# The first job's third output moved ahead of TensorE's expert loop, and the blank rows written later from another buffer

## Chip, cores and metric

One core of one Trainium2 chip runs the whole program. The metric is the device time of one execution in microseconds (us); lower is better. The kernel before was timed in three runs.

## What is computed

The reference is pooled attention followed by a mixture of experts in which each token goes to one expert:

```python
k_p = k.reshape(B, H, Sp, pool, D).mean(axis=3)       # B=8, H=8, S=576, D=64, pool=8: 72 keys
v_p = v.reshape(B, H, Sp, pool, D).mean(axis=3)
attn = softmax(scale * q @ k_p.T) ;  x = attn @ v_p    # x: 4608 tokens of 512
e_idx = argmax(x @ w_gate) ;  gate_w = softmax(x @ w_gate)[e_idx]
eom = sigmoid(x @ w_output_gate)
out[mask] = gate_w * eom * (relu(x[mask] @ w1[e]) @ w2[e])   # for each of 8 experts e
```

## The kernel before

The program has two phases. The first is one scheduled stream (the TileContext): 36 tiles of 128 tokens go through scores, softmax and values, and for each group of four tiles the routing computes where each token's row belongs. GpSimd (POOL) scatters every row into a DRAM tensor `xs`, sorted by expert (`place_ids`, L489); the region of expert e starts at row e * STRIDE. The order of all this is written out by hand: `at(step, f, ...)` puts a function into a plan, and a step stands for half a tile (steps 0 to 38). Functions of one step run in the order in which they were entered.

Three of these functions matter here. `gather_early` (step BEFORE = 31) waits until the scatters of the first six groups have landed and then has SyncE (SP) load the first 384 rows of expert 0 back from `xs` (`load_rows`, four DMAs, L102). `turn_x` (from step TURNS = 34) transposes these rows on VectorE (L107, called from L527). `blank_rows` (steps 28.5 to 32, eight DMAs of SP, L224) writes 128 blank rows in front of each later expert's region and at the end of `xs`; their source is `blank`, a part of the weight staging buffer `stage[5]`, which POOL clears at step 26. SP handles its list in order, so a wait in front of one DMA holds back all behind it. `stage_in` loads pieces of weights (512 KB) into the six staging buffers, piece 5 into `stage[5]` at step 33. A second cleared buffer, `tail`, lies in `kbd[0]` (a keys buffer whose last reader is tile 31) and is cleared at step 34; `blank_tail` (L447) scatters it behind the first expert's rows at the end of the phase.

At the end of the first phase TensorE already runs the first layer of expert 0's first job and five eighths of its first output (`first_layer`, the list TAIL). A barrier of all engines (L1664) separates the phases.

The second phase is a `Block` with one program per engine, in which lists of jobs are worked off. A job is three or two tiles (384 or 256 rows) of one expert: the first layer `l1` (L1185, 96 matmuls in eight chunks f), the relu on ScalarE (L1266) and a remainder on VectorE (L1408, `low`), and the second layer `l2` (L1139, 24 matmuls per tile). The three accumulators `p_h` rotate over the chunks, so chunk f waits for the remainder of chunk f - 3 (semaphore `hl`). VectorE scales the outputs (`output`, L1400), POOL scatters them. TensorE's program starts at slot CODE = 159 of a block of 256 instructions. It finishes the first job's outputs of tiles 0 and 1 (L1236, the matmuls of L703), adds to `l1` in `begin`, and enters `looped`: `one_expert` for expert 0, then a loop of four passes over pairs of experts (L903). The first job goes through the same loop body as the others: `started` gives done > 0 for it, the body skips `l1`, waits for `y`, waits for its own outputs with `pre` (L1215), adds 2 to `l2`, and skips the two calls of `l2` for tiles 0 and 1 to reach the one for tile 2:

```python
            if done is not None:
                with eng.If(done > 0):
                    eng.wait_ge(q["pre"], 2)
                    eng.nop().then_inc(q["l2"], 2)
                with eng.Else():
                    l2(e, u, 0, job)
                    l2(e, u, 1, job)
```

In this data expert 0 has two jobs of three tiles and one of two. In the profiled run the word `rows[E + 1]` is 3, so the first job is a begun one (the nop of L1216 is in the trace).

Of the kernel before, what the change touches and what calls it, by code (L numbers as in the profile page):

```python
# [13 lines left out]
I32 = mybir.dt.int32  # L14
# [7 lines left out]
N, DM, FF, E = B * S, H * D, 1024, 8  # L22
P = 128
# [3 lines left out]
STAGES = 6  # L27
# [12 lines left out]
SENT = ROW - GATES  # L40
# [42 lines left out]
TURN = 5  # L83
FIRST = 2
CODE = 159


class Shared:
# [32 lines left out]
def attention_and_routing(ctx, tc, sh, qT, kT, v, wg, wst, xs):  # L121
    nc = tc.nc
# [5 lines left out]
    def const(shape, dt, name):  # L128
        return cp.tile(shape, dt, tag=name, name=name)
# [8 lines left out]
    kbd = [const([P, 4, 2 * KEYS], F32, f"kbd{j}") for j in range(2)]  # L138
# [3 lines left out]
    rev, first, running = const([P, E], F32, "rev"), const([P, E], F32, "first"), const([P, E], F32, "running")  # L142
# [71 lines left out]
        nc.vector.tensor_copy(running, first)  # L214
        nc.vector.tensor_copy(order, rev)

    blank = sh.stage[STAGES - 1][:, 0:SENT]

    def prepare_blank():
        nc.gpsimd.memset(blank, 0.0)  # L220
# [220 lines left out]

    close = []
    tail_at = const([P, 1], I32, "tail_at")
    tail = kbd[0].rearrange("p c n -> p (c n)")[:, 0:SENT]

    def blank_tail():
        ins = nc.gpsimd.indirect_dma_start(out=xs, out_offset=bass.IndirectOffsetOnAxis(ap=tail_at, axis=0),  # L447
                                           in_=tail.bitcast(I32), in_offset=None)
        for name in ("ids", "blank"):
            tc.declare_no_dep(ins.ins, group=name, reason="rows behind the first expert's")  # L450
        tc.add_to_no_dep_group("ids", ins.ins)
# [122 lines left out]
    def at(step, f, *args):  # L574
        plan.setdefault(step, []).append((f, args))
# [42 lines left out]
    for g in range(len(GROUPS)):  # L618
        at(sum(GROUPS[:g + 1]) + 2, lambda g: queue.append([route(g), 0, g]), g)

    at(26, prepare_blank)
    for e in range(E):
        at(28.5 + 0.5 * e, blank_rows, e + 1)
    at(34, nc.gpsimd.memset, tail, 0.0)
    at(BEFORE, gather_early)
    for k in range(WIDE):
        at(TURNS + 0.5 * k, turn_x, k)
# [138 lines left out]
def experts(st, nc, sh, wst, xs, out):  # L766
# [26 lines left out]
    q = {k: st.enter_context(nc.semaphore("m_" + k)) for k in names}  # L793
# [8 lines left out]
    def counts(v):  # L802
        trips = nc.s_assert_within(v & 15, 0, 12, skip_runtime_bounds_check_because="four bits, of 36 tiles")
        pairs = nc.s_assert_within((v >> 4) & 3, 0, 2, skip_runtime_bounds_check_because="two bits")
        return trips, pairs

    def one_expert(eng, v, e, job, slot, body, late):
        trips, pairs = counts(v)
        single, after_trips, after_pairs = v & 64, v & 128, v & 256
        for size, n in ((3, trips), (2, pairs)):  # L810
            with eng.If(n > 0):
                with eng.Fori(0, n) as i:
                    each(e, size, i, n, job, slot, body, trips, pairs, single, after_trips, after_pairs, late)
            job = eng.snap(job + n)
            slot = eng.snap(slot + n * size)
        return job, slot, trips, pairs, single

    def each(e, size, i, n, job, slot, body, trips, pairs, single, after_trips, after_pairs, late):
        body(e, size, job + i, slot + i * size, single, i if size == 3 else i + trips,
             (n - 1 - i) * 128 + after_trips if size == 3 else after_pairs - (n - 1 - i) * 256,  # L820
             1 - (n - 1 - i) - (pairs if size == 3 else 0), late, n - 1 - i)
# [52 lines left out]
    def whole(eng, r, most):  # L874
        return nc.s_assert_within(eng.snap(r), 0, most, skip_runtime_bounds_check_because="there are at most 50 slots")  # L875
# [19 lines left out]
    def looped(eng, rows, body, alone, marked):  # L895
        few = eng.alloc_register("few")
        eng.reg_mov(few, 1 - ((rows[1] >> 6) & 1))
        job, slot = one_expert(eng, rows[0], 0, 0, 0, body, None)[:2]
        begun = [eng.alloc_register(k) for k in ("job_r", "slot_r")]
        words = [eng.alloc_register(f"word{k}") for k in range(2)]  # L900
        for r, x in zip((*begun, words[0]), (job, slot, rows[1])):
            eng.reg_mov(r, x)
        with nc.Fori(0, E // 2, engines=[eng.engine]) as g:  # L903
            at = begun
            for k in range(2):
                e = nc.s_assert_within(2 * g + k, 0, E - 1, skip_runtime_bounds_check_because="experts in order")
                v = nc.s_assert_within(eng.snap(words[k]), 0, 1023, skip_runtime_bounds_check_because="counts of a few bits each")
                at = far_expert(eng, v, (e, (k + 1) % 2), whole(eng, at[0], 50), whole(eng, at[1], 56), body,
                                lambda: eng.reg_load(words[1 - k], sh.table[0:1, bass.ds(e + 2, 1)]), alone,
                                [] if k else marked, few)  # L910
            for r, x in zip(begun, at):
                eng.reg_mov(r, x)
        return whole(eng, begun[0], 50), whole(eng, begun[1], 56)

    def begin(eng, rows, names, step=None):
        with eng.If(rows[E + 1] > 2):
            for name, n in names:
                eng.nop().then_inc(q[name], n)
        if step is not None:
            with eng.Else():  # L920
                step(0)
                step(1)
                with eng.If((rows[E + 1] & 1) > 0):
                    step(2)
# [4 lines left out]
    def started(e, size, rows, nth):  # L929
        return rows[E + 1] - 2 - nth if e == 0 and size == 3 else None  # L930
# [192 lines left out]
    def _(eng):  # L1123
        mm = nc.tensor.matmul

        def parity(e):
            return e[1] if isinstance(e, tuple) else e % 2

        def split_by(e, n):
            eng.wait_ge(q["wl"], 8 * (e[0] + 1) + n - EARLY)  # L1130

        def l2(e, u, k, job, bank=None):
            w, to = sh.w2[parity(e)], p_y[k if bank is None else bank]
            for f in range(8):
                if k == 0:
                    eng.wait_ge(q["hl"], 8 * job + f + 1)
                o = DM * f
                for part, h in ((0, 0), (1, 0), (0, 1)):
                    i = mm(to, ht[:, h, f, P * k:P * k + P], w[:, part, o:o + DM],  # L1139
                           start=(f == 0 and part == 0 and h == 0), stop=(f == 7 and h == 1))  # L1140
            i.then_inc(q["l2"], 1)
# [31 lines left out]
        def l1(e, size, u, job, n):  # L1173
            w = sh.w1[parity(e)]
            eng.wait_ge(q["xl"], u + size)
            if e:
                split_by(e, 4)
            for f in range(8):
                if f >= 3:
                    eng.wait_ge(q["hl"], 8 * job + f - 2)  # L1180
                for d in range(4):
                    o = FF * d + P * f
                    to, terms = p_h[f % 3][:, 0:n], [(part, xt[:, x, d, 0:n]) for part, x in ((0, 0), (0, 1), (1, 0))]
                    for k, (part, x) in enumerate(terms):
                        i = mm(to, w[:, part, o:o + P], x, start=(d == 0 and k == 0), stop=(d == 3 and k == len(terms) - 1))  # L1185
                i.then_inc(q["l1"], 1)
# [13 lines left out]
            l2(e, u, 1, job, 2)  # L1200

        def body(e, size, job, u, single, nth, more, last, late, left):
            done = started(e, size, rows, nth)
            if done is not None:
                with eng.If(done <= 0):
                    l1(e, size, u, job, size * P)
            elif size == 3:
                l1(e, size, u, job, size * P)
            else:
                two(e, u, job, more)  # L1210
                return
            eng.wait_ge(q["y"], u + 2)
            if done is not None:
                with eng.If(done > 0):
                    eng.wait_ge(q["pre"], 2)  # L1215
                    eng.nop().then_inc(q["l2"], 2)  # L1216
                with eng.Else():
                    l2(e, u, 0, job)
                    l2(e, u, 1, job)
                    with eng.If(more > 0):  # L1220
                        eng.wait_ge(q["xl"], u + size + 3)
            else:
                if e:
                    split_by(e, 8)
                l2(e, u, 0, job)
            if done is None:
                l2(e, u, 1, job)
                with eng.If(more > 0):
                    eng.wait_ge(q["xl"], u + size + 3)
            l2(e, u, 2, job)  # L1230

        eng.addr_align(256, offset=CODE, max_nops=0)
        eng.nop().then_inc(q["l2"], 1)
        for k, f0 in ((0, F0), (1, 0)):
            for f in range(f0, 8):
                i = output_chunk(nc, sh, f, p_y[k], k)  # L1236
            i.then_inc(q["pre"], 1)
        rows = table(eng)

        begin(eng, rows, [("l1", 8)])  # L1240
        job, slot = looped(eng, rows, body, one, marked)
        eng.wait_ge(q["xl"], slot + 2)
        for k in ("xs", "xu"):
# [450 lines left out]
```

## Time and profile before

| | us |
|---|---|
| runs | 604.02, 605.68, 602.70 |
| median of the runs | 604.02 |
| profiled execution, device time | 600.8 |
| span of the profiled execution | 599.1 |
| TensorE busy (PE, 3345 matmuls) | 565.9 (94% of the span) |
| weight loads (PEld) | 512.2 (86%) |
| VectorE (DVE) busy | 338.8 (57%) |
| ScalarE (ACT) busy | 256.5 (43%) |
| GpSimd (POOL) busy | 227.3 (38%) |
| read from and written to HBM | 75.07 MB and 22.59 MB |

All times in the trace are us from the start of the span. A name that ends in q (PEldq, DVEq, SPq) is the sequencer of an engine, which hands instructions to the engine and can be ahead of it; a branch, a semaphore wait or a DMA issue stands there. The arrow in brackets of a timeline row names what ended the idle time before it; "issue" says that the profile shows nothing that the engine waited for.

### The profile page before, as it was taken

The page shows a single profiled execution, that of the slowest core. Times are in us where ns is not written, and L with a number is a line of the kernel's source. Part 1 is how long each engine was busy: PE and PEld are TensorE (multiplying, and loading weights), DVE is VectorE, ACT ScalarE, POOL GpSimd, SP SyncE. Part 2 cuts the span into 40 slices and gives each one's busy share as a digit, 9 for nine tenths or more (in the row PEclk, how much of TensorE's full clock was granted, in tenths as well). Part 3 has the DMA queues.
Part 4 walks back from the last instruction along what each step waited for, and adds up shares of the span by engine and source line. Part 5 has one row for each costly group of instructions (what it writes and reads, how often), then busy time and mean ns, then how long its engine had stood idle before and what let it go on. Part 6 is the DMA issues. An engine that isn't in the chain of part 4 may idle for free. (4 is left out here: it accounts for less than half of the span.)

```text
span 599.1 us, 12079 instructions
## 1 busy us (share of the span) xinstructions
PE 565.9 (94%) x3345; PEld 512.2 (86%) x3346; DVE 338.8 (57%) x777; ACT 256.5 (43%) x693; POOL 227.3 (38%) x351
## 2 busy tenths in 40 slices
PE   2999999987987999999999999999999999999996
PEld 2899898976975989889899898999898898989895
DVE  4687888986877533679384623457244741323231
ACT  2988989886343311558162311335042420202020
POOL 3937889933534513143323112311221422213131
PEclk9999999998997999999999999999999999999999
DMA  8867799888457721469855513074223303020112
GB/s 329 318 231 292 284 345 376 294 248 233 170 144 233 242 53 37 125 210 357 251 176 193 173 48 71 18 228 140 84 50 110 76 0 94 10 70 18 53 35 71
DMA packets 49694, 97.16 MB, mean 162 GB/s; under 512 B 7054, under 2 KB 31630, under 8 KB 47824
## 3 DMA queue, kind: packets, MB, share of 16 engines
q1 hardware_dynamic: 41648, 77.14, 40.3%
q0 software_dynamic: 7968, 19.24, 8.9%
q14 instruction: 60, 0.49, 0.3%
q8 instruction: 18, 0.29, 0.2%
HBM read 75.07 MB, written 22.59 MB: 163 GB/s over the span
## 5 line engine op out<-in xcount | busy, mean ns | idle before, releaser
L1266 ACT ACTIVATE ht<-p_h 128x384 fp32r<-128x384 f32 (+1 forms) x104 | 46.8, 450 | 241.6 <-PE p_h L1185 241.4
L1608 POOL DMA_INDIRECT out<-rows,dst x41 | 42.5, 1037 | 203.7 <-DVE rows L1400 196.1
L1185 PE MATMUL p_h<-xt,w1b 128*128 128x384 f32 (+1 forms) x672 | 107.9, 320 | 1.5 <-DVE ht L1408 0.9
L1408 DVE SCALAR_TENSOR_TENSOR ht<-p_h,ht 128x384 fp32r<-128x384 f32 (+1 forms) x104 | 52.1, 503 | 100.8 <-ACT ht L1266 94.5
L1185 PEld LDWEIGHTS p_h<-xt,w1b 128*128 128x128 f32 x672 | 106.6, 189 | 2.8 <-DVE ht L1408 1.2
L1139 PE MATMUL p_y<-w2b,ht 128*128 128x512 f32 x456 | 104.8, 390 | 0.0
L1139 PEld LDWEIGHTS p_y<-w2b,ht 128*128 128x128 f32 x456 | 85.4, 188 | 17.5
L1139 PE MATMUL p_y<-w2a,ht 128*128 128x512 f32 x384 | 90.9, 397 | 3.7 <-issue 3.7
L1139 PEld LDWEIGHTS p_y<-w2a,ht 128*128 128x128 f32 x384 | 73.6, 193 | 19.4 <-issue 4.2
L1185 PE MATMUL p_h<-xt,w1a 128*128 128x384 f32 (+1 forms) x576 | 85.8, 309 | 0.8 <-DVE ht L1408 0.8
L1185 PEld LDWEIGHTS p_h<-xt,w1a 128*128 128x128 f32 x576 | 85.0, 190 | 1.7 <-DVE ht L1408 1.2
L1400 DVE TENSOR_SCALAR rows<-p_y,sc 128x512 f32<-128x512 f32 x37 | 27.7, 751 | 101.1 <-PE p_y L1139 100.0
L327 ACT ACTIVATE p<-p_h,m 128x72 f32<-128x72 f32 x288 | 72.2, 378 | 16.3 <-DVE m L321 16.1
L347 PE MATMUL p_y<-vbd,pT 128*128 128x162 f32 (+3 forms) x400 | 68.8, 323 | 3.1 <-DVE xg L370 3.0
L1585 POOL DMA_INDIRECT xm<-xs,src x54 | 56.1, 1039 | 26.3 <-POOL src L1581 14.5
L347 PEld LDWEIGHTS p_y<-vbd,pT 128*128 128x128 f32 (+1 forms) x400 | 55.2, 183 | 6.6 <-DVE xg L370 3.5
L489 POOL DMA_INDIRECT xs<-xg,where x36 | 37.2, 1032 | 29.6 <-issue 9.2
L260 POOL TENSOR_TENSOR kq<-kq 128x288 f32<-128x288 f32 (+1 forms) x63 | 40.5, 672 | 12.7 <-DMA kq<-kT 12.0
L315 PE MATMUL p_h<-kbd,q_even 128*128 128x144 f32 (+1 forms) x160 | 29.5, 314 | 11.6 <-DMA q_even<-qT 8.9
L370 DVE TENSOR_TENSOR xg<-p_y,grec 128x400 f32<-128x400 f32 x72 | 36.2, 503 | 1.6
L336 PE MATMUL ptr<-ident,p 128*128 128x128 f32 x180 | 33.1, 283 | 3.6 <-ACT pT L337 1.9
L321 DVE TENSOR_REDUCE m<-p_h 128x4 f32<-128x288 f32 x72 | 32.4, 450 | 6.8 <-PE p_h L315 6.3
(190 smaller groups left out, 663.9 us busy)
## 6 DMA issues: line engine op xcount, KB each, us to landing
stage<-wst SPq DMA_DIRECT2D x64, 512.0 KB, 5.0
kq<-kT SPq DMA_DIRECT2D x7, 1152.0 KB, 13.8
rows<-xs SPq DMA_DIRECT2D x40, 192.0 KB, 6.8
rows<-v SPq DMA_DIRECT2D x8, 768.0 KB, 5.6
kq<-qT SPq DMA_DIRECT2D x4, 1152.0 KB, 9.8
rows<-v SPq DMA_DIRECT2D x8, 512.0 KB, 6.2
rows<-xs SPq DMA_DIRECT2D x64, 64.0 KB
q_even<-qT SPq DMA_DIRECT2D x3, 1152.0 KB, 8.9
```

Of the source, the lines that this page charges most:

```text
L260: nc.gpsimd.tensor_tensor(k[:, :, 0:w], k[:, :, 0:w], k[:, :, w:2 * w], op=ALU.add)
L327: nc.scalar.activation(pt[i % 3][:, o:o + KEYS], sv[:, h], AF.Exp, bias=m[:, h:h + 1])
L336: nc.tensor.transpose(tr[:, P * c:P * c + P], pt[i % 3][:, o:o + P], ident)
L347: nc.tensor.matmul(av[r0:r0 + n, o:o + COLS * (k1 - k0)], pT[:, BLOCKS[0] * a + c, r0:r0 + n], vbd[b % 2][:, k0:k1].rearrange("p h f -> p ...
L370: nc.vector.tensor_tensor(view(xg[g][:, j], h0, [[H, D + 16], [1, n]]), avv[:, :, 0:D + 16].rearrange("p h f -> p f h"), grec[g][:, j, h0: ...
L489: ins = nc.gpsimd.indirect_dma_start(out=xs, out_offset=bass.IndirectOffsetOnAxis(ap=where, axis=0), in_=x.bitcast(I32), in_offset=None)
L1139: i = mm(to, ht[:, h, f, P * k:P * k + P], w[:, part, o:o + DM], start=(f == 0 and part == 0 and h == 0), stop=(f == 7 and h == 1))
L1185: i = mm(to, w[:, part, o:o + P], x, start=(d == 0 and k == 0), stop=(d == 3 and k == len(terms) - 1))
L1266: act(ht[:, 0, f, 0:n], p_h[f % 3][:, 0:n], AF.Relu).then_inc(q["hh"], 1)
L1408: nc.vector.scalar_tensor_tensor(ht[:, 1, f, 0:n], src, 0.0, ht[:, 0, f, 0:n].bitcast(F32), op0=ALU.max, op1=ALU.subtract).then_inc(q["hl" ...
L1585: nc.gpsimd.indirect_dma_start(out=xb[:, k].bitcast(I32), out_offset=None, in_=pairs_of, in_offset=bass.IndirectOffsetOnAxis(ap=src[:, k:k ...
L1608: nc.gpsimd.indirect_dma_start(out=out, out_offset=bass.IndirectOffsetOnAxis(ap=dst[:, k:k + 1], axis=0), in_=yb[2 if k == size - 1 else k ...
```

## The change

Two edits. In the second phase, TensorE does the third output of the begun first job ahead of the loop: if the word is above 2, it adds 8 to `l1` and 2 to `l2` and runs `l2(0, 0, 2, 0)` at once; the loop over expert 0's jobs then starts at job 1, and its body has no case for a begun job. The loop over pairs of experts is pinned to slot HEAD = 142 of its block of 256 instructions. In the first phase, the blank buffer and the tail buffer become one (`kbd[0]`), cleared once at step 33, and the eight writes of blank rows move from steps 28.5 to 32 to steps 33.5 to 37.

```diff
+HEAD = 142
...
-    blank = sh.stage[STAGES - 1][:, 0:SENT]
+    blank = kbd[0].rearrange("p c n -> p (c n)")[:, 0:SENT]
...
-    tail = kbd[0].rearrange("p c n -> p (c n)")[:, 0:SENT]
...
-                                           in_=tail.bitcast(I32), in_offset=None)
+                                           in_=blank.bitcast(I32), in_offset=None)
...
-    at(26, prepare_blank)
+    at(33, prepare_blank)
     for e in range(E):
-        at(28.5 + 0.5 * e, blank_rows, e + 1)
-    at(34, nc.gpsimd.memset, tail, 0.0)
+        at(33.5 + 0.5 * e, blank_rows, e + 1)
...
-    def one_expert(eng, v, e, job, slot, body, late):
+    def one_expert(eng, v, e, job, slot, body, late, begun=0):
...
         for size, n in ((3, trips), (2, pairs)):
-            with eng.If(n > 0):
-                with eng.Fori(0, n) as i:
+            i0 = begun if size == 3 else 0
+            with eng.If(n - i0 > 0):
+                with eng.Fori(i0, n) as i:
...
-        job, slot = one_expert(eng, rows[0], 0, 0, 0, body, None)[:2]
+        first = nc.s_assert_within((rows[E + 1] >> 1) & 1, 0, 1, skip_runtime_bounds_check_because="one bit")
+        job, slot = one_expert(eng, rows[0], 0, 0, 0, body, None, first)[:2]
...
-        with nc.Fori(0, E // 2, engines=[eng.engine]) as g:
+        with nc.Fori(0, E // 2, engines=[eng.engine], head_slot={eng.engine: HEAD}) as g:
...
         def body(e, size, job, u, single, nth, more, last, late, left):
-            done = started(e, size, rows, nth)
-            if done is not None:
-                with eng.If(done <= 0):
-                    l1(e, size, u, job, size * P)
-            elif size == 3:
-                l1(e, size, u, job, size * P)
-            else:
+            if size == 2:
                 two(e, u, job, more)
                 return
+            l1(e, size, u, job, size * P)
             eng.wait_ge(q["y"], u + 2)
-            if done is not None:
-                with eng.If(done > 0):
-                    eng.wait_ge(q["pre"], 2)
-                    eng.nop().then_inc(q["l2"], 2)
-                with eng.Else():
-                    l2(e, u, 0, job)
-                    l2(e, u, 1, job)
-                    with eng.If(more > 0):
-                        eng.wait_ge(q["xl"], u + size + 3)
-            else:
-                if e:
-                    split_by(e, 8)
-                l2(e, u, 0, job)
-            if done is None:
-                l2(e, u, 1, job)
-                with eng.If(more > 0):
-                    eng.wait_ge(q["xl"], u + size + 3)
+            if e:
+                split_by(e, 8)
+            l2(e, u, 0, job)
+            l2(e, u, 1, job)
+            with eng.If(more > 0):
+                eng.wait_ge(q["xl"], u + size + 3)
             l2(e, u, 2, job)
...
-        begin(eng, rows, [("l1", 8)])
+        with eng.If(rows[E + 1] > 2):
+            eng.nop().then_inc(q["l1"], 8)
+            eng.nop().then_inc(q["l2"], 2)
+            l2(0, 0, 2, 0)
         job, slot = looped(eng, rows, body, one, marked)
```

## Rows read from the trace of the kernel before

**Rows 1.** The page's 40 slices: granted TensorE clock, in tenths.

```profile
PEclk9999999998997999999999999999999999999999
```

**Rows 2.** Waits of PE over the whole span: total, times, longest.

```profile
PE p_y L1139 <- issue: 3.7, 1, 3.7
PE p_y L347 <- DVE xg L370: 3.0, 1, 3.0
...
PE p_y L703 <- PEq L1664: 1.8, 1, 1.8
```

**Rows 3.** Waits of PE from 195 to 599 us.

```profile
PE p_h L1185 <- DVE ht L1408: 1.8, 2, 0.9
```

**Rows 4.** Timeline of PE, 140 to 262 us: start, length, instructions, idle before.

```profile
176.03 7.80 PE L703 MATMUL p_y<-w2a,ht 128*128 128x512 f32 x33 [1.80 <-PEq L1664]
187.57 8.14 PE L1139 MATMUL p_y<-w2a,ht 128*128 128x512 f32 x24 [3.74 <-issue]
195.55 16.83 PE L1185 MATMUL p_h<-xt,w1a 128*128 128x384 f32 x96
...
240.09 11.07 PE L1139 MATMUL p_y<-w2a,ht 128*128 128x512 f32 x48
```

**Rows 5.** Sequencer instructions of L1214 and L1216: ns min/median/max, first and last start.

```profile
L1214 PEldq COMPARE_BRANCH  x3: 77/218/3439, 181.4 to 209.2; - x3
...
L1216 PEldq EVENT_SEMAPHORE  x1: 51/51/51, 183.9 to 183.9; - x1
```

**Rows 6.** Windows table: length, PE, PEld, DVE, ACT, POOL, PEclk, DMA, GB/s.

```profile
187.57:192.60 5.03, 5.03 (x12) 4.01 (x13) 4.11 (x5) 3.44 (x4) 3.89 (x4) 0.50 0.34 81
```

**Rows 7.** Timeline of DVE, 136.9 to 143.5 us.

```profile
138.66 0.45 DVE L370 TENSOR_TENSOR xg<-p_y,grec 128x240 f32<-128x240 f32 x1
142.40 0.71 DVE L107 STREAM_TRANSPOSE rows<-rows 128x512 f32<-128x512 f32 x1 [3.28 <-DMA rows<-xs]
```

**Rows 8.** Timeline of SP's DMA issues, 118 to 148 us.

```profile
122.58 2.19 SPq L224 DMA_DIRECT2D xs<-stage  x3
133.50 2.07 SPq L102 DMA_DIRECT2D rows<-xs  x4
...
146.76 1.11 SPq L503 DMA_DIRECT2D stage<-wst  x2
```

**Rows 9.** Timeline of POOL, 117 to 139 us: the sixth group's last scatter.

```profile
123.62 1.34 POOL L489 DMA_INDIRECT xs<-xg,where  x1 [0.30 <-issue]
```

**Rows 10.** Issue to landing: scatters 110 to 128 and 150 to 159; L102; L224.

```profile
xs<-xg,where POOLq DMA_INDIRECT x4, 8.7
...
xs<-xg,where POOLq DMA_INDIRECT x4, 4.6
...
DMA to landing us min/median/max: 5.6/6.8/7.3
...
DMA to landing us min/median/max: 5.8/9.6/10.3
```

**Rows 11.** Timeline of DVE, 188 to 199 us.

```profile
188.43 0.69 DVE L1359 TENSOR_TENSOR xt<-p_h,xt 128x512 fp32r<-128x512 f32 x1 [0.66 <-ACT xt L1255]
...
192.97 1.41 DVE L1400 TENSOR_SCALAR rows<-p_y,sc 128x512 f32<-128x512 f32 x2
195.75 0.75 DVE L1400 TENSOR_SCALAR rows<-p_y,sc 128x512 f32<-128x512 f32 x1 [1.37 <-PE p_y L1139]
198.38 0.56 DVE L1408 SCALAR_TENSOR_TENSOR ht<-p_h,ht 128x384 fp32r<-128x384 f32 x1 [1.88 <-ACT ht L1266]
```

**Rows 12.** Timeline of ACT, 186 to 199 us.

```profile
190.18 1.05 ACT L1262 ACTIVATE w2b<-stage 128x1024 fp32r<-128x1024 f32 x1
197.85 0.49 ACT L1266 ACTIVATE ht<-p_h 128x384 fp32r<-128x384 f32 x1 [6.62 <-PE p_h L1185]
```

**Rows 13.** Sequencer instructions of L903, the head of the loop over pairs.

```profile
L903 PEldq MOVE  x1: 29/29/29, 247.4 to 247.4; - x1
```

**Rows 14.** Waits of SP's queue, 168 to 176 us.

```profile
SPq L1664 <- DMA xs<-kbd,tail_at: 2.1, 1, 2.1
```

## Prediction

> **What bounds the kernel now.** TensorE works in 94% of the span, so I looked first for the places where it does not. The clock line of the page [rows 1] shows two dents, in the 10th slice (135 to 150 us) and in the 13th (180 to 195 us). TensorE's waits name what lies there [rows 2]: 3.7 us in front of L1139 that end by "issue", 3.0 us in front of L347 that end by a DVE normalisation, 1.8 us at the barrier between the phases. From 195 us on TensorE waits 1.8 us for DVE in two pieces [rows 3] and hardly otherwise, so from there to the end the time is matmuls: what is won earlier stays won, if nothing new comes late, and an edit that slowed the matmul stream would cost in full.
>
> The first place is the start of the second phase [rows 4]. The remaining 33 matmuls of the first job's outputs run from 176.03 for 7.80 us, to 183.83; the 24 matmuls of its third output begin at 187.57. The sequencer tells what happens between [rows 5]: the wait on TensorE's own outputs (L1216) ends at 183.9, when they are done, and then comes a branch of L1214, the jump over the two outputs that need not be computed, of 3439 ns. Such branches stand elsewhere too (median 218 ns), but there the sequencer is ahead of the matmuls; here the wait has made it give up its lead, so the branch is fully exposed. [...] So 24 matmuls take 8.14 us, where 48 of the same kind at full clock take 11.07 [rows 4], that is 5.54 for 24.
>
> The second place is in the first phase. DVE stands still for 3.28 us until 142.40, waiting for the rows that `gather_early` loads, before it can transpose them [rows 7]. It then normalises late, and TensorE's 3.0 us wait follows from that [rows 2]. Backwards: SP has issued six of the eight blank writes by 124.77, but the loads only from 133.50 to 135.57 [rows 8], because they wait for the sixth group's scatters. The last of these is issued by POOL at 123.62 [rows 9]. The four of this stretch take 8.7 us to land (median); four that run from 150 to 159 us, with no blank writes around, take 4.6 [rows 10].
>
> **The change part by part.**
>
> *Third output ahead of the loop.* The wait for `pre` is gone, and so is the taken branch behind it; the new code follows the 33 matmuls in a straight line. Cost of the new instructions: one untaken branch and two increments of about 50 ns each, as at L1216 [rows 5], with the sequencer ahead of 7.80 us of matmuls: nothing. If a fetch were late in the straight line, the bound is the same 3.4 us again; below zero it cannot go, since the same 24 matmuls must run. The third output then runs from 183.83 at full clock and ends at 183.83 + 5.54 = 189.4, where before it ended at 195.55, when job 1's first layer starts [rows 4]. That is 6.2 us: 3.7 of pause and 2.5 of clock.
>
> Who is late next? Job 1's first layer needs the third tile's remainder, done at 188.43 + 0.69 = 189.1 [rows 11]: just in time, 0 to 0.1 us. Its chunks last 16.83/8 = 2.10 us [rows 4], so the fourth can start at 189.4 + 6.3 = 195.7, once DVE has done the remainder of the first. DVE has its two outputs done at 192.97 + 1.41 = 194.4; the third (0.75), whose 1.37 us wait for TensorE is now gone, ends at 195.1 to 195.6 (its register work unseen, 0 to 0.5 us); the remainder (0.56) follows at 195.7 to 196.2 [rows 11]. ACT is no limit: its split of weights ends at 191.2, and the first relu, which waited 6.62 us for TensorE [rows 12], can run at 191.5. So a new wait of 0 to 0.5 us appears in front of the fourth chunk. I take the upper end: the register work is certainly there, only its size is unseen. Sum of this part: 6.2 - 0.5 = 5.7 us, between 5.6 and 6.2.
>
> *Blocks and the pinned loop.* By my count of instructions (two per matmul, starting from slot 159) the loop over pairs starts at slot 143 of the fourth block now; HEAD = 142 puts it at the same place of the next one, so its inner branches keep their places. New is one jump over the padding when the loop is entered. The sequencer is there at 247.4 [rows 13], while the matmuls of that stretch run to 240.09 + 11.07 = 251.2 [rows 4]: 3.7 us of lead. Priced like L1214, 3.4 us, it is covered but leaves little lead; 0 to 0.8 us, and I take 0, as branches whose median is 0.2 us are the common case.
> [...]
>
> *Blank rows later.* Eight writes of 257 KB leave the stretch from 119 to 138 us. The scatters then share it with two 512 KB loads alone. I take their landing between 4.6 and 8.7 us [rows 10], so the last has landed at 128.2 to 132.3. The loads take 2.07 us to issue [rows 8] and 5.6 to 7.3 to land [rows 10]; from first issue to last landing it was 142.4 - 133.5 = 8.9. They are there at 137.1 to 141.2. DVE wants them at 139.1 (138.66 + 0.45, [rows 7]). The gain is therefore the whole 3.28 us at one end and 1.2 at the other; zero if something else holds the scatters. I take 3.3, because the stretch from 150 to 159 is the nearer row: blank writes are missing in both. DVE runs without a pause behind it, so TensorE, ACT and POOL, who all waited for DVE, move by the same amount; the lower clock of that dent costs nothing of its own, as TensorE had slack beside DVE.
>
> Where do the writes go? Their source is now cleared in POOL's queue among the scatters of the seventh group; one clearing replaces two, and POOL had idle time there: nothing. On SP they stand behind the loads and weight piece 5, which no longer waits for `stage[5]`. Two follow at once, six behind the next weight load, which waits for a split that DVE had finished by 147.9 [rows 8]. At 0.8 us each (6.45 us for the eight) the last is issued by 152.7 and, at the longest landing of 10.3 us [rows 10], down by 163. What ends the phase is the scatter of the tail rows, for which SP waits 2.1 us shortly before the barrier [rows 14], at about 173. So 10 us of cover remain; without it every microsecond would go on the barrier. The barrier's own 1.8 us stays.
>
> **Sum.** 5.7 + 3.3 = 9.0 us. Against the profiled execution: 600.8 - 9.0 = 591.8. The median of the runs is 3.2 us above that execution; I subtract from the median: 604.0 - 9.0 = 595.0 us.
>
> **Rivals.** (A) The loads come no earlier, because the scatters are slow for another reason (the weight loads, or their own descriptors). For: there are weight loads in that stretch too. Against: the 4.6 us row. Then 604.0 - 5.7 = 598.3. (B) TensorE's fetch stall only moves: into the third output or onto the entry of expert 0's loop. For: the code around it is new and expert 0's loop lies elsewhere. Against: no jump and no wait remains there. Then 604.0 - 3.3 = 600.7. (C) Slower: the loop over pairs now lies one block further on, and a branch in it misses in every pass with no lead. One exposure costs what L1214 did, 3.7 of pause and 2.5 of clock, 6.2 us; from the second on it eats the 9.0. With three, once in each later pass: 604.0 - 9.0 + 18.6 = 613.6. For: that price was paid once. Against: [rows 3], no such wait in the same loop before, whose slots are kept. (D) Neither edit does anything: 604.0. That the new branch is not taken can be left out: L1216, which only a begun job reaches, is in the trace.
>
> **How the numbers follow.** Forecast 0.72, A 0.12, B 0.08, C 0.04, D 0.04. The largest gain from the bounds is 6.2 + 3.3 = 9.5; with the 1.3 us by which the fastest run lies under the median, 593.2, and I go to 592.5 for the clock of the first dent. Upwards the range goes to B, 600.7. Half a per cent, about what a measurement of this kernel can tell from no change, is 3.0 us, so faster means below 601.0: forecast, A and half of B, 0.88. Same: the other half of B and D, 0.08. Slower: C, 0.04.
>
> **What would show it.** In the trace after: no idle in front of the third output's 24 matmuls, which take about 5.5 us, and no lower clock there; a wait of at most about half a microsecond for DVE a few chunks into job 1; DVE's transposes without a wait for rows; SP's loads issued at about 129, blank writes behind them; the barrier 3.3 us earlier, its wait still for the tail. I am wrong if a new "issue" wait stands in front of L1139 or L1185, if the loads still leave at 133, or if waits appear after 250 us in the loop over pairs.

## Result and the profile after

The kernel after takes 608.92 us (median of six runs, 606.68 to 610.04) beside 603.80 for the kernel before in the same comparison: ratio 1.0078, 95% interval 1.0053 to 1.0103. It is slower by about 5 us where 9 us less was forecast. The profiled execution took 608.39 us with a span of 606.6 (before: 600.8 and 599.1).

First the stretch that the edit of the third output aimed at, in the timeline of PE after (start, length, instructions, idle before):

```profile
176.82 7.77 PE L702 MATMUL p_y<-w2a,ht 128*128 128x512 f32 x33 [1.45 <-PEq L1652]
184.43 5.60 PE L1140 MATMUL p_y<-w2a,ht 128*128 128x512 f32 x24
190.00 6.54 PE L1186 MATMUL p_h<-xt,w1a 128*128 128x384 f32 x36
197.13 10.69 PE L1186 MATMUL p_h<-xt,w1a 128*128 128x384 f32 x60 [0.60 <-issue]
```

The third output has no pause in front and takes 5.60 us instead of 8.14 [rows 4]. From the start of the 33 matmuls to the start of job 1's first layer it is 190.00 - 176.82 = 13.18 us; before it was 195.55 - 176.03 = 19.52 [rows 4]: 6.3 us less. The small wait of 0.60 a few chunks into job 1 is there too. So this part did what was forecast, and still the program is longer. From the start of job 1's first layer to the end of the span it is 606.6 - 190.0 = 416.6 us, where before it was 599.1 - 195.55 = 403.6. Thirteen microseconds came in behind the place that was changed. The waits of PE after, from 195 to 604 us, say where (total, times, longest; before: [rows 3]):

```profile
PE p_h L1186 <- issue: 9.7, 2, 9.1
PE p_h L1186 <- DVE ht L1396: 2.2, 2, 1.4
PE p_h L1162 <- issue: 0.3, 1, 0.3
```

The 9.1 us in the timeline of PE after, 280 to 312 us:

```profile
279.74 11.49 PE L1140 MATMUL p_y<-w2a,ht 128*128 128x512 f32 x50
300.34 11.84 PE L1186 MATMUL p_h<-xt,w1b 128*128 128x256 f32 x79 [9.11 <-issue]
```

This is the second pass of the loop over pairs, in front of expert 3's first job. What the sequencer did then is in its instructions after (ns min/median/max, first and last start):

```profile
L828 PEldq COMPARE_BRANCH  x8: 66/76/2915, 243.7 to 598.0; - x8
...
L835 PEldq COMPARE_BRANCH  x6: 68/72/5821, 255.6 to 598.7; - x6
...
L904 PEldq COMPARE_BRANCH  x5: 76/208/431, 243.0 to 600.0; - x5
```

L835 is `with eng.If(trips > 0)` in `far_expert`. Expert 3 has no job of three tiles, so the sequencer jumps over that body, and this one jump, which starts at 290.0, takes 5821 ns. The matmuls in the queue end at 291.2: the lead is 1.2 us, and 4.6 us of the jump lie open. The other 4.5 us of the wait are the way from the jump's target to the first matmul: up to the next branch (L843, at 299.3) the sequencer takes 3.4 us there, where the kernel before takes 0.9 (from 293.6 to 294.4). L828 in the first pass (2915 ns) is the jump to the path for an expert with a single job; there the lead covers all but 0.3 us. L904 is the head of the loop; it has five branches where the kernel before has four. The fifth is the jump over the padding.

Of the two queues that the page names instruction, q14 moved 60 packets before and after, and q8 seven more after; the row of q8 in the table of DMA queues of before, then of after (packets, MB):

```profile
q8 instruction: 18, 0.29, 0.2%
```

```profile
q8 instruction: 25, 0.41, 0.3%
```

And the pause costs clock. The clock line of the page of after, and the windows table for the stretch of the low clock (columns as in [rows 6]):

```profile
PEclk9899999999999999999799999999999999999999
```

```profile
294.92:305.16 10.24, 4.82 (x22) 4.82 (x23) 0.62 (x2) 1.44 (x2) 3.53 (x7) 0.50 0.06 16
```

The dents of [rows 1] in slices 10 and 13 are gone and there is a new one in slice 20: 4.82 us of matmuls at 0.50, which would take 2.4 at full clock. The price of the pause that this jump begins is 9.1 + 2.4 = 11.5 us. (The dent in slice 2 belongs to an early pause at 22 us. It stands in some of the profiles and not in others, with and without either edit.)

The first phase, timeline of SP's issues after, 118 to 150 us:

```profile
130.94 2.13 SPq L103 DMA_DIRECT2D rows<-xs  x4
134.41 0.82 SPq L503 DMA_DIRECT2D stage<-wst  x2
139.97 0.95 SPq L225 DMA_DIRECT2D xs<-kbd  x2
```

The loads leave ahead of the blank writes and earlier than in [rows 8], although the work before them was late in this execution: POOL's scatter that starts at 133.0 us before starts at 137.0 here.

### The profile page after: what moved, and what is told of

Its sections match the earlier page's. It is cut to its first block, busy times and chain, and to the rows that moved or that the text cites. A ratio compares the mean times of both kernels' runs of the same rounds, so it can differ in the third digit from the quotient of the medians.

```text
span 606.6 us, 12067 instructions
## 1 busy us (share of the span) xinstructions
PE 567.3 (94%) x3345; PEld 512.3 (84%) x3346; DVE 338.5 (56%) x777; ACT 256.5 (42%) x693; POOL 226.9 (37%) x350
## 4 chain that ended last, share of the span: by engine, by line
PE 52%; issue 2%; DVE 1%; DVEq 0%; POOL 0%; ACT 0%; POOLq 0%; ACTq 0%
PE p_y L1140 26%; PE p_h L1186 25%; PE p_h L1162 1%; PE p_h L1168 0%; DVE w2b L1354 0%; DVE ht L1396 0%; POOL out L1596 0%; DVE xt L1347 0%; DVE rows L1388 0%; DVE flat L1382 0%; ACT ht L1263 0%; DVEq L1442 0%; DVEq L875 0%; DVEq L865 0%; DVEq L868 0%
## 5 line engine op out<-in xcount | busy, mean ns | idle before, releaser
L1186 PE MATMUL p_h<-xt,w1b 128*128 128x384 f32 (+1 forms) x672 | 110.0, 324 | 10.5 <-issue 9.1
L1186 PEld LDWEIGHTS p_h<-xt,w1b 128*128 128x128 f32 x672 | 108.7, 193 | 11.9 <-issue 9.7
L1140 PE MATMUL p_y<-w2a,ht 128*128 128x512 f32 x384 | 88.4, 389 | 0.0
L1140 PEld LDWEIGHTS p_y<-w2a,ht 128*128 128x128 f32 x384 | 71.8, 188 | 14.7
```

## Experiments

Each ratio is against runs of the kernel before on the same chip. Line numbers shift by a few between kernels. Slots are written block:slot in blocks of 256, the unit by which the kernel aligns TensorE's program (`addr_align(256, offset=CODE, ...)`), blocks numbered from 0 (the prediction's "fourth block" is block 3 here), and are my count of instructions. The expectations use letters: M, that the place of the loop within its block decides, to two slots; B, a loss in the first phase; S, that expert 0's loop now makes one pass instead of two and so brings less code; J, that the jump over the padding makes the loss. T and the numbered J's are explained where they first stand.

**Two slots (M).** The kernel after with HEAD = 140.

```diff
-HEAD = 142
+HEAD = 140
```

> The changed kernel with HEAD = 140 instead of 142: the loop over pairs is still entered by the jump over the padding, but lies two slots lower in its block, as in the kernel before. Theory M (missing block): in the first pass expert 1 takes the single-job path; with HEAD = 142 that path begins at slot 1 of the block after next, so the block between is never brought in, and the jump of L835 in the second pass (expert 3 has no job of three tiles) finds it missing: 9.1 us of wait and 10.2 us at half clock, some 11.5 us in all. With HEAD = 140 the path begins at slot 255 of that block and brings it in: no such wait, 608.9 - 11.5 = 597.4 us (595.5 to 599.5). Rival J (the jump into the loop itself loses what was fetched ahead, wherever it lands): the wait stays, 607 to 610. Rival B (the loss lies in the first phase, with the blank writes): 607 to 610 as well, but without the 9.1 us wait.

605.89 us, ratio 1.0066 (1.0043 to 1.0089). The sequencer's row:

```profile
L835 PEldq COMPARE_BRANCH  x6: 68/72/5765, 253.1 to 594.9; - x6
```

The wait stays at 8.3 us. M falls as it was put, with a border between slots 140 and 142.

**Without padding, first try.**

```diff
-CODE = 159
-HEAD = 142
+CODE = 116
+HEAD = 140
```

> The changed kernel with CODE = 116 and HEAD = 140: TensorE's second program starts 43 slots earlier, so the loop over pairs comes to lie at slot 140 of the fourth block of itself, as in the kernel before, and nothing is jumped over. Theory M and rival J both: no wait at L835, and the branch of L828 (2.9 us after the change) is short again: 597 us (595.5 to 599). Rival B: 607 to 610. If code116 and head140 agree within 1 us, the jump over the padding costs nothing by itself.

604.48 us, 1.0040 (1.0016 to 1.0063), L835 at 5941 ns. The edit did not do what was meant; the row of L904 still has its fifth branch:

```profile
L904 PEldq COMPARE_BRANCH  x5: 76/208/427, 240.3 to 595.4; - x5
```

Probably the padding's own branch takes a slot too, so that the head was just past the place and moved on by nearly a whole block; no run shows this. The loop is entered by a jump here as well, so the run cannot tell J from its rivals.

**One part alone: the blank rows.** The kernel before with the edits of the first phase.

```diff
-    blank = sh.stage[STAGES - 1][:, 0:SENT]
+    blank = kbd[0].rearrange("p c n -> p (c n)")[:, 0:SENT]
...
-    at(26, prepare_blank)
+    at(33, prepare_blank)
...
-        at(28.5 + 0.5 * e, blank_rows, e + 1)
-    at(34, nc.gpsimd.memset, tail, 0.0)
+        at(33.5 + 0.5 * e, blank_rows, e + 1)
```

> The kernel before with the blank rows' part alone: one buffer, cleared at step 33, writes at steps 33.5 to 37. By my prediction DVE no longer waits 3.28 us for the rows: 603.8 - 3.3 = 500.5 + 100 = 600.5 us (599.5 to 602.5). Rival B (the writes cost more in their new place, or the earlier part of the phase runs slower for them): first layer of the first job starts 1.1 us later than before, as in the profile of the changed kernel: 604.9 us or more.

597.86 us, 0.9933 (0.9905 to 0.9961). SP's issues, DVE's first transposition and two of PE's waits in this kernel:

```profile
129.09 2.22 SPq L102 DMA_DIRECT2D rows<-xs  x4
```

```profile
139.66 0.69 DVE L107 STREAM_TRANSPOSE rows<-rows 128x512 f32<-128x512 f32 x1
```

```profile
PE p_y L1137 <- issue: 2.8, 1, 2.8
...
PE p_y L347 <- DVE xg L370: 0.7, 1, 0.7
```

The loads leave at 129.09 instead of 133.50 [rows 8], the 3.28 us wait of [rows 7] is gone, the 3.0 us wait of TensorE [rows 2] has shrunk to 0.7, and the pause in front of the third output is still there, as it should be. This part gains 4.0 us by the ratio (2.3 to 5.7). B falls.

**The other part alone, with the pin.** The kernel after with the blank rows as before.

```diff
...
-    at(33, prepare_blank)
+    at(26, prepare_blank)
...
-        at(33.5 + 0.5 * e, blank_rows, e + 1)
+        at(28.5 + 0.5 * e, blank_rows, e + 1)
+    at(34, nc.gpsimd.memset, tail, 0.0)
```

> The changed kernel with the blank rows as before, so TensorE's part alone with HEAD = 142. Theory M: the third output starts at once (6 us gained) and L835 misses its block (11.5 us lost): 603.8 + 5.5 = 609.3 us (607.5 to 611). Rival B: 603.8 - 5.7 = 598.1 us.

611.22 us, 1.0147 (1.0110 to 1.0183). The wait for issue in front of expert 3 is 10.1 us. So the loss sits in the edits of TensorE's program, not in the first phase.

**Without the pin.** The kernel after without the pin, at two places of the program; with CODE = 116 the loop begins in another part of its block.

```diff
-        with nc.Fori(0, E // 2, engines=[eng.engine], head_slot={eng.engine: HEAD}) as g:
+        with nc.Fori(0, E // 2, engines=[eng.engine]) as g:
```

CODE = 116:

> The changed kernel with CODE = 116 and without the pin (no head_slot): by count the loop over pairs starts at slot 140 of the fourth block, as in the kernel before, and is entered in a straight line. In code116 the trace still had a taken branch of 326 ns in front of the loop, so the pin moved the loop by a whole block even there. Theory J (the jump over the padding enters a new block 0.6 us ahead of the next jump, L828; the block behind it is skipped, and L835 of the second pass needs it): no wait at L835, no long L828; blank_only was 597.9 with the third output's pause still in it, so 597.9 - 4 = 594 us (592 to 596). Rival S (the shorter run through expert 0's loop, one pass instead of two, leaves other blocks behind, with or without the jump): the 9 us wait at L835 stays, 602 to 606.

CODE = 159:

> The changed kernel without the pin and with CODE = 159: the loop over pairs starts 43 slots later in the fourth block and is entered in a straight line. Theory J: no wait at L835, as in nopin116; 594 us (592 to 597), the same as nopin116 within 1.5. If the place of the loop within its block matters by itself (what the pin is for), this one is slower than nopin116 by 3 us or more, with branches above 2 us in the loop over pairs. Rival S: 602 to 606.

593.43 us, 0.9862 (0.9840 to 0.9884), and 594.12 us, 0.9880 (0.9851 to 0.9909). Sequencer and waits (195 to 604 us) with CODE = 159:

```profile
L828 PEldq COMPARE_BRANCH  x8: 66/76/359, 239.7 to 582.4; - x8
...
L835 PEldq COMPARE_BRANCH  x6: 67/72/228, 251.4 to 583.0; - x6
```

```profile
PE p_h L1186 <- DVE ht L1396: 1.7, 2, 0.9
PE p_h L1186 <- issue: 0.6, 1, 0.6
```

Neither long jump is left, and 18 packets are moved as before. S falls, since expert 0's loop makes one pass here too. Both kernels are faster than before and after, and have the lowest ratios of this study.

**The jump alone, in the kernel before.** Nothing of the change but the pin: once so that the loop is entered by a jump into the next block, once with a pad within the block.

```diff
-CODE = 159
+CODE = 162
+HEAD = 142
...
-        with nc.Fori(0, E // 2, engines=[eng.engine]) as g:
+        with nc.Fori(0, E // 2, engines=[eng.engine], head_slot={eng.engine: HEAD}) as g:
```

> The kernel before, with nothing changed but CODE = 162 and the pin HEAD = 142: the loop over pairs comes to lie where it does in the changed kernel and is entered by the jump over the padding; TensorE runs expert 0's loop as before, twice. Theory J: L828 takes 2.5 to 3 us, L835 over 5 us in the second pass, 9 us of wait and a dent in the clock: 602.7 + 11 = 614 us (611 to 616). Rival S: 602 to 604.

And with CODE = 159:

> The kernel before with the pin HEAD = 142 and CODE = 159: by count there is one slot of padding, so the loop is entered by a taken branch that stays in its block. Theory J (a new block is needed for the loss): like before, 602.7 us (601.5 to 604). Rival T (any taken branch between the hint L1193 and the jump L828 spoils the fetch ahead): L828 above 2 us, and L835 too: 606 to 614.

The jump: 612.22 us, 1.0198 (1.0154 to 1.0243). The hop: 603.10 us, 1.0017 (0.9997 to 1.0037). Sequencer and timeline of the first, sequencer of the second:

```profile
L829 PEldq COMPARE_BRANCH  x8: 66/76/3023, 247.0 to 600.0; - x8
...
L836 PEldq COMPARE_BRANCH  x6: 67/72/5939, 259.0 to 600.6; - x6
```

```profile
303.36 1.01 PE L1186 MATMUL p_h<-xt,w1b 128*128 128x256 f32 x3 [9.04 <-issue]
```

```profile
L829 PEldq COMPARE_BRANCH  x8: 66/76/351, 248.4 to 591.3; - x8
...
L836 PEldq COMPARE_BRANCH  x6: 68/72/220, 260.1 to 591.9; - x6
...
L904 PEldq COMPARE_BRANCH  x4: 76/212/234, 292.9 to 593.2; - x4
```

The whole loss appears in the kernel before once its loop is entered by a jump into the next block. J holds so far. The hop has only four branches of L904, the first at 292.9, so it entered its loop without a taken branch, other than expected: what a jump within the block would cost (rival T) no run shows. What is left is why the bill comes in the second pass, 50 us later; the last six kernels ask that.

**The third output alone, without the pin.** The kernel after with blank rows as before and no `head_slot` (both diffs are shown above), CODE = 159.

> The third output ahead of the loop alone: blank rows as before, no pin (CODE = 159). The step of the prediction for this edit says 5.7 us less than before (5.6 to 6.2), so 0.990 to 0.991 of the kernel before; with the 5.9 us that the blank rows alone gave, the two would add up to 11.6, where the kernel with both and no pin gave 8.4 to 8.8 less. If the edits share a gain, this one shows 2.5 to 3 us less than before (0.995). The first wait in front of L347's successor, 2.7 to 3.3 us near 145, must still be there, and the third output must start without a pause.

597.38 us, 0.9921 (0.9888 to 0.9953): 4.8 us less, between 2.8 and 6.7. Timeline of PE:

```profile
177.29 7.77 PE L704 MATMUL p_y<-w2a,ht 128*128 128x512 f32 x33 [2.33 <-PEq L1654]
184.90 5.60 PE L1142 MATMUL p_y<-w2a,ht 128*128 128x512 f32 x24
190.44 6.51 PE L1188 MATMUL p_h<-xt,w1a 128*128 128x384 f32 x36
197.57 2.70 PE L1188 MATMUL p_h<-xt,w1a 128*128 128x384 f32 x14 [0.61 <-DVE ht L1398]
```

With the 4.0 us of the blank rows (the 5.9 in the expectation compares medians taken on different chips) the parts add up to 8.8; the two kernels with both show 0.0138 and 0.0120 of 602 us, 8.3 and 7.2. By the trace the third output's stretch is as short here as with both edits (190.44 - 177.29 = 13.15 us), so no shared gain shows; the ratios alone leave room for one.

**Which code the first pass brings.** Pinned kernels with the loop at other places of block 4; each is the kernel after with one number changed.

```diff
-HEAD = 142
+HEAD = 100
```

> The kernel after with HEAD = 100 instead of 142: the pin and its taken jump over the padding into the fourth block stay, but the loop over pairs lies 42 slots earlier in that block, so that by my count the target of L835's jump (5:210) and the start of the path for an expert with one job (5:215) both lie in the block right behind the head; with HEAD = 142 they lie at 5:252 and 6:1. Theory J2 (the jump in brings one block, and the next jump, taken 0.6 us later, leaves out the block between): no block is left out, L835 in the second pass stays under 0.5 us, no 9 us wait for issue near 290, 594 to 598 us. Rival J1 (a taken jump into a block not yet there is enough by itself, whatever lies behind): L835 stays at 5.8 us, the 8 to 9 us wait stays, 605 to 609 us. J2 has against it that HEAD = 140, where the same path starts at the last slot of the fifth block, kept the wait.

HEAD = 20:

> The kernel after with HEAD = 20: the same jump over the padding, the loop over pairs 122 slots earlier, so that the jump to L835's target and the one to the single-job path end well inside the fifth block (5:130 and 5:135) and what follows them lies there too. Theory J2: as head100, no long L835, 594 to 598 us. If head100 keeps the wait and this one does not, what counts is how much of a block lies behind the target. Rival J1: the wait stays, 605 to 609 us.

597.12 us, 0.9896 (0.9859 to 0.9932), and 597.76 us, 0.9918 (0.9886 to 0.9950). Sequencer and timeline with HEAD = 100:

```profile
L828 PEldq COMPARE_BRANCH  x8: 66/73/2958, 241.1 to 587.0; - x8
...
L835 PEldq COMPARE_BRANCH  x6: 68/72/229, 256.2 to 587.6; - x6
...
L850 PEldq COMPARE_BRANCH  x2: 179/1783/3387, 251.9 to 465.6; - x2
```

```profile
256.89 5.39 PE L1186 MATMUL p_h<-xt,w1a 128*128 128x384 f32 x22 [2.66 <-DVE w2a L1354]
```

The 9 us wait is gone although the jump over the padding is still there, so J1, that such a jump is enough by itself, falls. L828 takes 3 us as before, and another jump is now long: L850, from the end of the single-job path to the next expert, 3.4 us with 2.7 open (4.6 and 3.8 with HEAD = 20). The wait is put down to DVE, but the sequencer reached these matmuls only when L850 had ended at 255.3. By its trace this costs 2.7 us and some clock (the clock line of its page has an 8 in slice 18, 253 to 268 us); the ratios of these two stand a little behind those without a pin (0.9862 and 0.9880), and of the intervals only those of HEAD = 20 and the unpinned kernel with CODE = 116 do not overlap.

Two values nearer to 142, and one above it. HEAD = 136:

> The kernel after with HEAD = 136: by my count the target of L835's jump lies at 5:246 and the single-job path begins at 5:251, five slots before the end of the block behind the head (HEAD = 140, which kept the 8 to 9 us wait: 5:250 and 5:255; HEAD = 100, which had it no more: 5:210 and 5:215). Theory J2 (whole blocks of 256 slots, the one that is left out is what costs): the single-job path now certainly touches the fifth block, so L835 in the second pass stays under 0.5 us and the wait near 290 is gone; L828 still takes near 3 us, and since the path crosses into the sixth block at once, up to 3 us more may lie open near 250; 594 to 600 us. HEAD = 140 then kept its wait because the count is one or two slots off. Rival J3 (what is brought begins at the target, not at a block's border, or much of a block must lie behind it): L835 still misses, the 8 to 9 us wait stays, 604 to 608 us.

HEAD = 128:

> The kernel after with HEAD = 128: by my count L835's target lies at 5:238 and the single-job path begins at 5:243 (HEAD = 136, which kept the wait: 5:246 and 5:251; HEAD = 100, which had none: 5:210 and 5:215). If the wait of 136 came from a count that is up to some ten slots short, the wait is gone here, 595 to 600 us; if it stays, 603 to 608 us, the border lies at least 12 slots ahead of the end of the block by my count.

HEAD = 180:

> The kernel after with HEAD = 180: the jump over the padding into the fourth block stays, the loop over pairs begins in the upper half of that block, and by my count L835's target lies at 6:34 and the single-job path at 6:39, both in the sixth block; the fifth is left out as with HEAD = 142, but L835 does not go there. Theory J2 (L835 misses because its target lies in the block that was left out): L835 in the second pass stays under 0.5 us, no 8 to 9 us wait near 290, L828 still near 3 us, 593 to 598 us unless the three-tile body of a later pass misses when it runs into the fifth block. Rival J4 (a head in the upper half of a block, or the jump by itself, makes the loss): the wait stays, 603 to 608 us.

604.45 us, 1.0046 (1.0024 to 1.0069); 610.21 us, 1.0092 (1.0047 to 1.0137, of two runs); 610.28 us, 1.0086 (1.0052 to 1.0121). All three keep the wait. Sequencer with HEAD = 136, then with HEAD = 180:

```profile
L835 PEldq COMPARE_BRANCH  x6: 68/72/5869, 252.2 to 593.2; - x6
...
L850 PEldq COMPARE_BRANCH  x2: 184/243/302, 251.0 to 471.2; - x2
```

```profile
L835 PEldq COMPARE_BRANCH  x6: 68/72/8578, 257.6 to 600.7; - x6
```

HEAD = 180 refutes J2 as I had put it: L835's target and the single-job path lie in the same block there, and the jump takes 8.6 us. So it is not that just the target's block was left out. Two readings remained: a block left out anywhere makes the code behind it count for nothing when the loop comes back to its head (J6), or the half of the block in which the loop begins decides (J4).

**A gap by itself.** HEAD = 20, whose loop begins in the lower half and had no such wait, with 131 slots that are never run between L835's target and the single-job path, so that by my count the first pass skips block 5.

```diff
-HEAD = 142
+HEAD = 20
+GAP = 130
...
         with nc.body(name + "_on", valid_engines=[eng.engine]):
-            eng.br(name + "_pairs")
+            if hints:
+                eng.br_eq(eng.to_reg(pairs), 77, on_true=name + "_gap", on_false=name + "_pairs")
+            else:
+                eng.br(name + "_pairs")
+        if hints:
+            with nc.body(name + "_gap", valid_engines=[eng.engine]):
+                for _ in range(GAP):
+                    eng.nop().then_inc(q["l2"], 1)
+                eng.br(name + "_pairs")
```

> The kernel after with HEAD = 20 (as head20, which had no 9 us wait), and 131 slots that are never run (a branch that is never taken leads to them) between L835's target and the single-job path of the pairs' first expert: by my count the target stays at 5:130, the path moves from 5:135 to 6:12, so that the first pass leaves out the fifth block. Theory J6 (the block left out in the first pass is what costs, wherever the loop begins): L828 near 3 us as before, L835 in the second pass 5 to 9 us, the 8 to 9 us wait near 290 is back, about 25 instruction packets, 604 to 610 us. Rival J4 (the half of the block in which the loop begins decides): no such wait, L835 under 0.5 us, 594 to 600 us.

604.39 us, 1.0037 (1.0020 to 1.0054). Sequencer and timeline:

```profile
L836 PEldq COMPARE_BRANCH  x6: 68/72/5969, 253.0 to 594.1; - x6
```

```profile
296.78 7.45 PE L1195 MATMUL p_h<-xt,w1b 128*128 128x256 f32 x47 [8.42 <-issue]
```

With the gap the long L835 (here L836) and the 8.4 us are back, with 25 packets against 21 in HEAD = 20. So J4 falls: the loop begins in the lower half here, and what was added is the gap. The loop is half a block longer as well, but by my count it spans seven blocks, as it does without the pin at CODE = 159, where no such wait stands.

## Why the prediction was wrong

**Third output ahead of the loop: right.** The stretch shrank by 6.3 us (forecast 6.2), the new wait is 0.60 (forecast 0 to 0.5), alone it gives 4.8 (2.8 to 6.7; forecast 5.7). The 2.5 us of clock in the sum are what the traces show: 8.14 us at the clock of [rows 6] became 5.60. Rival B does not hold for the places it named: with the pin taken out, no stall replaces the old one.

**Blank rows later: right.** Loads at 129.09 against "about 129", DVE's wait gone, 4.0 us alone (2.3 to 5.7; forecast 3.3). The last blank write begins at 151.5 us in the kernel after (forecast: issued by 152.7), and the barrier does not come to wait for them.

Together the two give 7.2 to 8.3 us where the sum said 9.0. In the profile of the unpinned kernel with CODE = 159 the timeline of PE shows one thing that the sum does not have:

```profile
172.83 9.40 PE L702 MATMUL p_y<-w2a,ht 128*128 128x512 f32 x33 [1.90 <-PEq L1652]
```

The barrier is 3.2 us earlier (172.83 beside 176.03), as forecast, but the 33 matmuls behind it took 9.40 us instead of 7.80 [rows 4], 1.6 us more; the clock line of its page has an 8 in this stretch (slice 12, 162.5 to 177.3 us), where the line of before [rows 1] has a 9. Job 1's first layer starts at 187.51, 8.0 us earlier than before, of the 8.1 by which this span is shorter. The longer 33 matmuls are in some profiles (9.37 us without the pin and with CODE = 116) and not in others (7.77 in the third output alone), and with CODE = 116 the interval of the ratio reaches 9.0 us, so I don't put the whole difference of the medians down to it.

**Blocks and the pinned loop: this step failed.** It priced one jump, the one over the padding, at 0 to 0.8 us, took 0, and said that the inner branches "keep their places". The padding's jump is indeed cheap (L904, 326 ns in the profiled run). What it cost was the two jumps behind it:

- L828, 0.7 us later, leads to the path for a single job. In four kernels whose loop is entered without a jump (before, the hop, and the two with both edits and no pin) it takes 0.35 to 0.36 us; in the kernel before a packet of q8 begins at 243.9, 6.0 us after the prefetch hint (L1193, 237.9) and 4.0 us ahead of L828. In all that are entered by the jump, L828 takes 2.7 to 3.1 us, and in the kernel after the first packet behind the hint (L1194, 233.4) begins at 243.9, when L828 has begun (243.7). The hint comes 9.6 us ahead of the jump (243.0), so the jump itself cannot be what keeps a packet back until then. The lead of 3.7 us [rows 13] that I had found was used up here, so far without harm.
- With HEAD = 142 the first pass then leaves out, by my count, the block behind the head. When the loop returns to its head, L835 takes 5.8 us with a lead of 1.2, and seven more packets of about 16 KB are moved (25 packets, 0.41 MB, beside 18 and 0.29). That a gap does this is shown by the last experiment (5969 ns, 25 packets); that block 5 is the one left out with HEAD = 142 rests on the count.

So "no such wait in the same loop before, whose slots are kept" was the false argument. The slot of the head does not tell what a branch will cost: HEAD = 142 cost 2% in the kernel before when the loop was entered by the jump, and nothing clear of noise when it was not. The count behind it was off as well: recounted, the loop of the kernel before begins at 3:140, not at slot 143. The hop, pinned to slot 142 and entered without a jump, fits that. By the runs with HEAD = 140 and 136 this made no difference.

Nor does the distance of a jump in blocks. By my count L828 leads two blocks on with HEAD = 142, and took 2915 ns; it leads only to the next block with HEAD = 100 and 20, and took 2958 and 2742 ns; in the kernel without the pin and with CODE = 159 it leads two blocks on, and took 359. The runs show the packets and the long jumps, and not what code is at hand when a branch is reached.

**Rivals.** The outcome is nearest to C, whose chance was 0.04: a loop one block further on, with a branch in it that misses. The number was wrong twice: one miss and not three, but 11.5 us instead of 6.2. I took L1214's 3.4 us as the price of a missed jump; L835's is 5.8, and a further pause follows on the way behind it, in which another packet begins (296.5 us).

**What stays open.** With HEAD = 128, 136 and 140 the single-job path begins, by my count, 13, 5 and 1 slots before the end of block 5; yet these kernels behave like those in which it begins in block 6 (short L850, long L835). Whether the count, or the handling of a block's last slots (near to J3), is the reason, no run here decides. Nor is it shown why no packet follows the hint in the kernel after until L828 has begun. In the unpinned kernel with CODE = 159 the single-job path begins, by the same count, at 5:42 with the head at 3:183 (371 slots behind it, as from 4:142 to 6:1), and L835 stayed at 0.23 us: there, by this count, leaving a block out in the first pass did not make L835 long, and no run shows why.

## To carry over

Price a change of code layout by the first way through the code, not by the slots: list every taken branch in the order in which the sequencer meets it, what code has been left out by then, and the lead of the sequencer at each. Here the jump over the padding took 326 ns where it stood, and the pause that begins at L835, when the loop came back, cost 11.5 us with its clock. Try the edit with and without the alignment: here the pin was the only part that lost.

## What was not expected of the hardware

The jump of L835, taken in front of expert 3, cost between 0.22 us and 8.6 us (HEAD = 180), by what had gone before and not by its own distance, which is the same in all kernels that differ by HEAD alone: 0.23 us with HEAD = 100 and 5.8 with 142. (The 0.07 us of its median are passes in which it is not taken.) The loop has, by my count, about 1560 slots, and in its third and fourth passes q8 moved no packet: the last begins at 295.2 us in the kernel before and at 362.8 in the kernel after, where the third pass begins at 392.1 and 399.1. In the pause of 9.1 us TensorE's clock fell to 0.50 for 10.24 us, 4.82 of them with matmuls, which made the 9.1 us into 11.5.
